# Where the tensor engine's operands begin in SBUF: every tile it reads is moved to 64 bytes past a multiple of 128

## The chip, the core and the metric

The kernel runs on one core of one Trainium2 chip. The core has a tensor engine (PE, whose weight loads the profile lists apart as PEld), VectorE (DVE), ScalarE (ACT), GpSimd (POOL) and SyncE (SP, here a queue that issues transfers). They run side by side and wait for each other through semaphores. SBUF is the on-chip memory of 128 partitions; a tile `[P, n]` takes n elements in every partition, at the same byte address in each. PSUM, in eight banks, takes what the tensor engine writes.

The metric is device time in microseconds (us). Before the change three runs took 1286.78, 1286.78 and 1286.92 us, so the median is 1286.78.

## The reference

An attention block and a gated feed-forward block read the same x, and a gate per token mixes them. Cut to what matters (S = 2048 tokens, D = 448, H = 16 heads of 28, F = 1792, all float32):

```python
g = sigmoid((x * gate_w).sum(-1, keepdims=True))
qkv = x @ wqkv                                  # D -> 3 D
scores = einsum("bhqd,bhkd->bhqk", q, k) * 28 ** -0.5
a = einsum("bhqk,bhkd->bhqd", softmax(scores), v) @ wo
gate = einsum("bsd,df->bsf", x, W_gate); up = einsum("bsd,df->bsf", x, W_up)
b = einsum("bsf,fd->bsd", gate * (gate > 0) * up, W_down)
out = g * a + (1 - g) * b
```

## The kernel before

**Numbers as a high and a low part.** The tensor engine multiplies in float32r here, a faster form of 4-byte operands that keeps fewer bits. Each float32 operand is therefore split into a rounded high part (ScalarE, or VectorE where `dve_high` is called) and the low rest (a subtraction on VectorE or GpSimd), and a product is summed from high x high, low x high and high x low. For the depth of 448 (three chunks of 128 and one of 64, in whose other 64 rows the low part is packed) that makes 11 matmuls for each output tile (`TERMS`).

**Stages.** Each engine's order of work is written out by hand.

1. Projections (first 150 us or so). `W` holds wqkv and the gate's column, split: seven rows of 1346 elements per partition, row a at byte 5384 a, which is 8 a past a multiple of 128. `qk` (line 337) uses 128 columns of W as weights and streams 512 tokens of X past them. `vproj` (line 355) holds 128 tokens of X as weights and streams 450 columns of W. Before them stand 11 warm-up matmuls on a tile of zeros, `warm` (lines 378 to 382). GpSimd then clears the padding columns of V (lines 390 to 392).
2. Attention with half of the feed-forward mixed in (to 1072 us). Strings of letters give the order of TensorE's work: `m` is a matmul of `smax` (line 181: scores for the row maximum that VectorE takes), `s` one of `scores` (line 207: the scores again, which ScalarE turns into exponentials in the tiles `P`), `x` one of `gu_mm` (line 506: gate and up, weights `wg`, moving X). Between two strings a block of `pv` (line 540) multiplies P by V: plain float32, 32 columns wide, two instructions for each product.
3. The end. The remaining gate and up products, `wout` (line 719: attention's output times `WO`) and `down` (line 764: hidden tiles `hh` times `WD`), each streaming 448 columns. 

**Where the tiles lie.** Pools are stacked in SBUF in the order in which they are opened, without gaps: from the low end `const`, `keep`, `vp`, then `qkv` (first stage), `att` (attention) or `ffn` (the end), and from the high end `fe`. The addresses of the program as built, in bytes of a partition:

| tiles that TensorE reads | used in line | begins at | past a multiple of 128 |
|---|---|---|---|
| X (in `keep`) | 337, 355, 506 | 17280, 25472 | 0 |
| V | 540 | 35840 | 0 |
| K, three of them | 181, 207 | 68608, 76800, 84992 | 0 |
| Q, three of them | 181, 207 | 101376, 109568, 117760 | 0 |
| P, eleven of them | 540 | 52224 to 183296 | 0 |
| W, row a | 337, 355 | 158720 + 5384 a | 8 a |
| wg, two of them | 506 | 192224, 199392 | 96 |
| WO, WD | 719, 764 | 35840, 56576 | 0 |
| on, hh | 719, 764 | 142592 and others | 0 |

A matmul reads a part of such a tile, and all of these parts lie a multiple of 128 bytes behind the tile's (or W's row's) beginning. The row maxima `m` (line 189, 16 small transposes) lie at 0 and 64 in turn.

Of the kernel before, what the change touches and what calls it, by code (L numbers as in the profile page):

```python
# [8 lines left out]
F32 = mybir.dt.float32  # L9
F32R = mybir.dt.float32r  # L10
BF16 = mybir.dt.bfloat16
# [7 lines left out]
P = 128  # L19
S = 2048  # L20
D = 448
# [7 lines left out]
TB = 512  # L29
# [2 lines left out]
SCALE = DH ** -0.5  # L32
VC = D + 2
NQ = 2 * D // P
WARM = 11

EARLY = (5, 5, 4, 4, 4, 3, 3, 3, 2, 2, 2, 2, 1, 1, 1, 1)
# [39 lines left out]
def gated_mix_kernel(ctx, tc, x, wq, wo, wgu, wd, out):  # L77
    nc = tc.nc
    ctx.enter_context(tc.manual_schedule(engines={ENG.PE, ENG.Activation, ENG.DVE, ENG.Pool, ENG.SP}))

    const = ctx.enter_context(tc.tile_pool(name="const", bufs=1))
    psum = ctx.enter_context(tc.tile_pool(name="psum", bufs=1, space=PSUM))
    dram = ctx.enter_context(tc.tile_pool(name="dram", bufs=1, space=DRAM))
    keep = ctx.enter_context(tc.tile_pool(name="keep", bufs=1))

    def f32(ap):
        return ap.bitcast(F32)
# [12 lines left out]
    def ps_x():  # L100
        return banks[turn("x", (4, 5))]
# [47 lines left out]
    V = vp.tile([P, 4, NK, 4, 32], F32, name="V")  # L149
# [63 lines left out]
    def xf(tb, b):  # L213
        return X[tb][b // 4][:, b % 4]
# [11 lines left out]


    with tc.tile_pool(name="qkv", bufs=1) as pa:
        W = pa.tile([P, 7, 2 * D + VC], F32R, name="W")

        def load_w(c):
            c0, c1 = c * 2 * GD, (c + 1) * 2 * GD if c < G + 1 else 2 * D + VC
# [5 lines left out]
        def split_w(wr, c0, c1):  # L238

            ways = [[(W[:, :, c0:c1], wr)]]  # L240
            if c0 < 2 * D:
                w, r = (ap.rearrange(f"p c {n} -> p c a j d", a=2, j=4)
                        for ap, n in ((W[:, :, c0:c1], "(j a d)"), (wr, "(a j d)")))
                ways = [[(w[:, :, a], r[:, :, a]) for a in range(2)]]
# [11 lines left out]
        def split_first(wr, xr):  # L256

            r = wr.rearrange("p c (a j d) -> p c a j d", a=2, j=4)
            w = W[:, :, :2 * GD].rearrange("p c (j a d) -> p c a j d", a=2, j=4)

# [50 lines left out]
        def ps_any(late=False):  # L311
            return (ps_x if late else turn("any", (ps_s, ps_s, ps_x, ps_x)))()

        def mix(n, among):

            k = len(among)
            for f, *a in among[k * n // NT:k * (n + 1) // NT]:
                f(*a)
# [5 lines left out]
        def st_tile(tb, c):  # L324
# [3 lines left out]
            if k < 15 and k % 5 > 2:  # L328
                return outs[k % 5 - 3]
            if c == NQ - 1 and tb == 0:  # L330
                return pair[0][:, 2:].bitcast(F32R)
            return pa.tile([P, 2, TB], F32R, name=f"st_{tb}_{c}", tag="st", bufs=3)

        def qk(tb, c, terms=TERMS, among=()):
            ps = ps_any(c == NQ - 1)
            for n, (a, b) in enumerate(terms):
                nc.tensor.matmul(ps, W[:, a, c * P:(c + 1) * P], xf(tb, b), start=(n == 0), stop=(n == NT - 1))  # L337
                mix(n, among)
            st = st_tile(tb, c)

            def send():
                act_high(st[:, 0], ps)
                low(st[:, 1], ps, st[:, 0])
                nc.gpsimd.dma_start(qk_d[:, c * P:(c + 1) * P, tb * TB:(tb + 1) * TB].rearrange("r d t -> d r t"),
                                    f32(st))


            sends.append(send)
            if (tb, c) != (0, NQ - 1):
                sends.pop()()  # L350

        def vproj(tb, t, among=()):
            ps = ps_any(tb == 0 and t > 1)
            for n, (a, b) in enumerate(TERMS):
                nc.tensor.matmul(ps[:, :VC], xf(tb, b)[:, t * P:(t + 1) * P], W[:, a, 2 * D:], start=(n == 0),  # L355
                                 stop=(n == NT - 1))
                mix(n, among)
            k = tb * 4 + t
            nc.scalar.activation(V[:, :, k, :, :DH], ps[:, :D].rearrange("p (g h d) -> p g h d", g=G, d=DH), AF.Copy)
            nc.scalar.activation(zt[:, k:k + 1], ps[:, D:D + 1], AF.Copy)  # L360
            if t == 3:
                for g in (2, 3):
                    nc.gpsimd.dma_start(v_d[g][:, k - 3:k + 1], V[:, g, k - 3:k + 1])
# [11 lines left out]
        x1 = load_x(1)  # L375


        warm = pa.tile([P, TB], BF16, name="warm")
        nc.vector.memset(warm, 0.0)
        ps = ps_x()  # L380
        for n in range(WARM):
            nc.tensor.matmul(ps, warm[:, :P], warm, start=True, stop=True)
# [38 lines left out]
        units = [(qk, 3, 1), (qk, 2, 2), (qk, 3, 2)]  # L421
        units += [(qk, tb, c) for c in range(3, NQ) for tb in range(NB - 1, -1, -1)]
        vs = [(vproj, tb, t) for tb in range(NB - 1, -1, -1) for t in range(4)]
        mixed = units[:2]
        units = units[2:]
# [43 lines left out]
    fe = ctx.enter_context(tc.tile_pool(name="fe", bufs=1, side="right"))  # L469
# [61 lines left out]
    OS, LS = {}, {}  # L531
# [24 lines left out]

    def spread(h):

        LS[h] = fe.tile([P, TB], F32, name=f"rb_{h}", tag="rb", bufs=1)
        for j in range(NB):  # L560
            nc.gpsimd.dma_start(LS[h][32 * j:32 * j + 32], l_d[h][j:j + 1].to_broadcast([32, TB]))

# [13 lines left out]
    def small_things(u):  # L576

        h, q = divmod(u, 4)

        if q == 0 and h and h + 2 < H:  # L580
            load_k(h + 2)
            load_q(h + 2)
        if u in (16, 32):
            g = u // 16 + 1
            nc.sync.dma_start(V[:, g % 2], v_d[g])
        if u == 2:
            pack_wo()
        if h and q == 2:
            row_sums(h - 1)
            spread(h - 1)  # L590
            summed.append(h - 1)
# [5 lines left out]
    for r, (order, nu) in enumerate(ROUNDS):  # L597
# [13 lines left out]
        for o in order:  # L611
# [16 lines left out]
            elif o == "x":  # L628
                i, half, k = passes.pop(0)
# [3 lines left out]
                if k == NT - 1:  # L633
                    i, half, ps = units.pop()
# [32 lines left out]
        for a in {i0, max(i0, (i0 + ni) // NK * NK)}:  # L667
            n = min(i0 + ni, (a // NK + 1) * NK) - a
# [132 lines left out]


    before(0, (spread, H - 1))
    before(1, (normalise, H - 1))
    for tb, load, split, at in ((0, 2, (3, 4), (5, 6, 7, 8)), (1, 5, (7, 9), (10, 11, 14, 14)), (2, 21, (23, 25), (28,) * 4),
                                (3, 35, (37, 39), (42,) * 4)):
        before(load, (fetch_o, tb))
        for k, i in enumerate(split):
            n = todo.index((down, i))
# [55 lines left out]
```

## Time and profile before

| | |
|---|---|
| median of the three runs | 1286.78 us |
| the profiled execution | 1284.91 us |
| its span, first to last instruction | 1283.1 us |
| instructions | 18205, of which 6687 matmuls |
| granted clock of TensorE | 1.000 |
| busy: PE, DVE, ACT, POOL | 100%, 70%, 61%, 29% of the span |

Each line of the groups by line names the source line, the engine, the operation, the tiles (written `out<-in`), the shapes and the count; then the busy time in us, the mean of one in ns, and the engine's idle time before them. The busy time of matmuls overlaps, since each begins before the last one has drained. The chain of work that ended last is followed back from the last instruction; in order of time each of its rows gives the start in us from the span's beginning, the length, and the engine and line that held the chain in that piece (`x22`: 22 instructions in a row).

### The profile page before, as it was taken

To read this page: it belongs to the slowest core of one execution; us is meant where nothing else is said; L and a number is where in the kernel's file an instruction comes from. 1 tells how busy PE (TensorE), PEld (TensorE's weight loads), DVE (VectorE), ACT (ScalarE), POOL (GpSimd) and SP (SyncE) were. 2 spreads that over 40 slices of the span, in tenths; PEclk is the share of its full clock that TensorE was granted. 3 is DMA by queue.
4 is the path that set the end of the run, shared out by engine and by line. 5 is a ranking of instruction groups with operands and counts; after the bars stand their busy time and mean duration, and the time that the engine had idled before them with its cause. 6 is when DMAs were issued, how large, how long until landed. Compare 5 with 4: busy or idle time off the path is not lost.

```text
span 1283.1 us, 18205 instructions
## 1 busy us (share of the span) xinstructions
PE 1277.6 (100%) x6687; PEld 922.8 (72%) x6687; DVE 895.1 (70%) x1364; ACT 777.0 (61%) x1424; POOL 370.4 (29%) x563
## 2 busy tenths in 40 slices
PE   9999999999999999999999999999999999999998
PEld 6888866677666676666766667766667666899997
DVE  6598768788777797777977778877779215663342
ACT  6212767687766786676867667766778773312121
POOL 3222222312323123323123331223231444551020
PEclk9999999999999999999999999999999999999999
DMA  9836443233144214231443423142331226634432
GB/s 321 290 151 244 133 137 86 71 79 98 60 132 146 74 43 114 71 103 50 116 119 120 109 70 77 43 115 66 108 105 36 83 83 204 218 109 135 143 104 78
DMA packets 53569, 148.89 MB, mean 116 GB/s; under 512 B 10024, under 2 KB 17128, under 8 KB 48872
## 3 DMA queue, kind: packets, MB, share of 16 engines
q1 hardware_dynamic: 36120, 98.34, 27.0%
q0 software_dynamic: 16928, 48.93, 10.6%
q8 instruction: 52, 0.85, 0.3%
q10 hardware_dynamic: 432, 0.46, 0.1%
q14 instruction: 37, 0.30, 0.1%
HBM read 102.06 MB, written 46.02 MB: 115 GB/s over the span
## 4 chain that ended last, share of the span: by engine, by line
PE 99%; DMA 0%; DVE 0%; issue 0%; ACT 0%; DVEq 0%
PE b L506 22%; PE b L207 19%; PE b L181 19%; PE b L540 17%; PE b L764 11%; PE b L337 5%; PE b L719 3%; PE b L355 3%; DMA wr<-wq 0%; PE b L189 0%; DVE W L129 0%; DVE X L129 0%; DVE y L770 0%; ACT X L123 0%; ACT W L123 0%
## 5 line engine op out<-in xcount | busy, mean ns | idle before, releaser
L182 DVE TENSOR_REDUCE mx<-b 128x1 f32<-128x512 f32 x1024 | 685.2, 688 | 27.5 <-PE b L181 20.4
L209 ACT ACTIVATE P<-b 128x512 f32<-128x512 f32 x840 | 493.0, 598 | 153.2 <-PE b L207 84.5
L506 PE MATMUL b<-X,wg 128*128 128x512 f32 (+1 forms) x1232 | 438.4, 400 | 0.0
L207 PE MATMUL b<-Q,K 114*128 114x512 f32 x1024 | 406.1, 397 | 0.0
L181 PE MATMUL b<-K,Q 112*128 112x512 f32 x1024 | 403.7, 397 | 0.0
L506 PEld LDWEIGHTS b<-X,wg 128*128 128x128 f32 (+1 forms) x1232 | 222.6, 189 | 58.0 <-issue 9.5
L207 PEld LDWEIGHTS b<-Q,K 114*128 114x128 f32 x1024 | 194.9, 190 | 53.1 <-issue 12.6
L181 PEld LDWEIGHTS b<-K,Q 112*128 112x128 f32 x1024 | 193.0, 189 | 49.1 <-DVE mx L182 2.6
L540 PE MATMUL b<-P,V 128*32 128x512 f32 x1680 | 188.2, 593 | 0.0
L132 POOL TENSOR_TENSOR wg<-wgr,wg 128x384 fp32r<-128x384 f32 x200 | 143.2, 732 | 9.8 <-issue 1.6
L764 PE MATMUL b<-WD,hh 128*128 128x448 f32 x672 | 141.1, 368 | 0.0
L540 PEld LDWEIGHTS b<-P,V 128*32 128x32 f32 x1680 | 52.6, 110 | 121.3 <-issue 118.7
L528 POOL DMA_DIRECT2D h_d<-h x56 | 31.4, 562 | 363.4 <-DVE h L522 311.7
L764 PEld LDWEIGHTS b<-WD,hh 128*128 128x128 f32 x672 | 126.1, 188 | 13.0
L209 ACT ACTIVATE V<-b 128x512 f32<-128x512 f32 x184 | 107.8, 599 | 41.3 <-PE b L207 26.7
L123 ACT ACTIVATE hh<-hr 128x512 fp32r<-128x512 f32 x56 | 35.2, 631 | 127.8 <-PE b L764 123.3
L129 DVE TENSOR_TENSOR hh<-hr,hh 128x512 fp32r<-128x512 f32 x56 | 50.7, 906 | 68.3 <-ACT hh L123 68.2
L337 PE MATMUL b<-X,W 128*128 128x512 f32 x308 | 84.1, 397 | 0.3 <-DVE X L129 0.2
L546 DVE TENSOR_TENSOR os<-b,os 128x512 f32<-128x512 f32 x16 | 11.1, 692 | 86.1 <-PE b L540 86.1
L337 PEld LDWEIGHTS b<-X,W 128*128 128x128 f32 x308 | 57.7, 189 | 15.3 <-DVE X L129 2.1
L555 POOL DMA_DIRECT2D l_d<-rs x16 | 9.0, 564 | 203.0 <-DVE rs L554 203.0
L544 DVE COPY os<-b 128x512 f32<-128x512 f32 x16 | 11.1, 691 | 78.5 <-PE b L540 78.5
(70 smaller groups left out, 709.8 us busy)
## 6 DMA issues: line engine op xcount, KB each, us to landing
wgr<-wgu SPq DMA_DIRECT2D x55, 512.0 KB
K<-qk_d SPq DMA_DIRECT2D x64, 224.0 KB
Q<-qk_d SPq DMA_DIRECT2D x64, 224.0 KB
h_d<-h POOLq DMA_DIRECT2D x56, 256.0 KB, 2.6
hr<-h_d SPq DMA_DIRECT2D x56, 256.0 KB
qk_d<-st POOLq DMA_DIRECT2D x21, 512.0 KB, 3.6
x_d<-X POOLq DMA_DIRECT2D x6, 1024.0 KB, 5.0
X<-x_d SPq DMA_DIRECT2D x24, 256.0 KB
```

What stands on the lines that cost most here:

```text
L129: nc.vector.tensor_tensor(dst, src, f32(high), op=OP.subtract)
L132: nc.gpsimd.tensor_tensor(dst, src, f32(high), op=OP.subtract)
L181: nc.tensor.matmul(ps, Q[h][:GD, u * P:(u + 1) * P], K[h % 3][:GD, c * TB:(c + 1) * TB], start=True, stop=True)
L182: nc.vector.tensor_reduce(MX[h][:, 4 * u + c:4 * u + c + 1], ps, axis=AX.X, op=OP.max)
L207: nc.tensor.matmul(ps, K[h % 3][:GD + 2, kt * P:(kt + 1) * P], Q[h][:GD + 2, j * TB:(j + 1) * TB], start=True, stop=True)
L209: nc.scalar.activation(PT[i][:, j], ps, AF.Exp, scale=SCALE)
L337: nc.tensor.matmul(ps, W[:, a, c * P:(c + 1) * P], xf(tb, b), start=(n == 0), stop=(n == NT - 1))
L355: nc.tensor.matmul(ps[:, :VC], xf(tb, b)[:, t * P:(t + 1) * P], W[:, a, 2 * D:], start=(n == 0), stop=(n == NT - 1))
L506: nc.tensor.matmul(ps, WS[i][rows, s, a], xf(i // NF, b)[rows], start=(n == 0), stop=(n == NT - 1))
L540: nc.tensor.matmul(po[32 * j:32 * j + 32], V[:, h // 4 % 2, i % NK, h % 4], p[:, j], start=(i == i0), stop=(i == i0 + ni - 1))
L719: nc.tensor.matmul(ps[:, :D], ON[tb][b // 4][:, b % 4, t * P:(t + 1) * P], WO[:, a], start=(n == 0), stop=(n == NT - 1))
L764: nc.tensor.matmul(ACC[i // NF][t][:, :D], HH[i][:, a, t * P:(t + 1) * P], WD[:, f, b], start=(f == 0 and n == 0), stop=(f == NF - 1 and n ...
```

## The change

No instruction is added, removed or put in another order. Four things change size or place:

- `const` gets a tile `pad` of 16 float32, 64 bytes, ahead of all others. Everything that is stacked from the low end moves up by 64 bytes: X, V, K, Q, P, WO, WD, on and hh begin at 64 past a multiple of 128.
- W's rows grow from 1346 to 1376 elements, 5504 bytes, which is 43 x 128. Every row then begins at 64. `vproj` names the 450 columns that it reads.
- `rb`, in the pool `fe`, is taken 8 elements longer. What is stacked from the high end moves down by 32 bytes, so wg goes from 96 to 64.
- `warm` has no tile of its own any more. It lies in the last quarter of V, which nothing has used yet at that time. Its size and type are as before. GpSimd's clearing of that quarter must now come behind the warm-up matmuls.

```diff
+WC = 1376
...
+    const.tile([P, 16], F32, name="pad")
...
-        W = pa.tile([P, 7, 2 * D + VC], F32R, name="W")
+        W = pa.tile([P, 7, WC], F32R, name="W")
...
-                nc.tensor.matmul(ps[:, :VC], xf(tb, b)[:, t * P:(t + 1) * P], W[:, a, 2 * D:], start=(n == 0),
+                nc.tensor.matmul(ps[:, :VC], xf(tb, b)[:, t * P:(t + 1) * P], W[:, a, 2 * D:2 * D + VC], start=(n == 0),
...
-        warm = pa.tile([P, TB], BF16, name="warm")
+        warm = V[:, 3, 0:2].rearrange("p k h d -> p (k h d)").bitcast(BF16)
...
-        LS[h] = fe.tile([P, TB], F32, name=f"rb_{h}", tag="rb", bufs=1)
+
+        LS[h] = fe.tile([P, TB + 8], F32, name=f"rb_{h}", tag="rb", bufs=1)[:, :TB]
```

## The prediction, made before the changed kernel ran

> **What bounds the kernel now.** I read the page's totals first, then the chain of work that ended last, then the groups of instructions by line and shape, and last the chain in order of time, piece by piece.
>
> ```profile
> span 1283.1 us, 18205 instructions
> ...
> PE 1277.6 (100%) x6687; PEld 922.8 (72%) x6687; DVE 895.1 (70%) x1364; ACT 777.0 (61%) x1424; POOL 370.4 (29%) x563
> ...
> PEclk9999999999999999999999999999999999999999
> ...
> PE 99%; DMA 0%; DVE 0%; issue 0%; ACT 0%; DVEq 0%
> PE b L506 22%; PE b L207 19%; PE b L181 19%; PE b L540 17%; PE b L764 11%; PE b L337 5%; PE b L719 3%; PE b L355 3%; DMA wr<-wq 0%; PE b L189 0%; DVE W L129 0%; DVE X L129 0%; DVE y L770 0%; ACT X L123 0%; ACT W L123 0%
> ```
>
> TensorE is the bound: 99% of the chain is matmuls, the clock is full in every slice, and no other engine is over 70%. So the time is the number of matmuls times the distance from one start to the next. A change that adds no instruction can move the time only by moving that distance. The counts come from the groups by line and shape:
>
> ```profile
> L506 PE MATMUL b<-X,wg 128*128 128x512 f32 x1136 | 421.9, 397 | 0.0
> L207 PE MATMUL b<-Q,K 114*128 114x512 f32 x1024 | 406.1, 397 | 0.0
> L181 PE MATMUL b<-K,Q 112*128 112x512 f32 x1024 | 403.7, 397 | 0.0
> L540 PE MATMUL b<-P,V 128*32 128x512 f32 x1680 | 188.2, 593 | 0.0
> L764 PE MATMUL b<-WD,hh 128*128 128x448 f32 x672 | 141.1, 368 | 0.0
> L337 PE MATMUL b<-X,W 128*128 128x512 f32 x308 | 84.1, 397 | 0.3 <-DVE X L129 0.2
> L355 PE MATMUL b<-W,X 128*128 128x450 f32 x176 | 46.9, 368 | 0.0
> L540 PE MATMUL b<-V 128*32 128x512 f32 x368 | 44.4, 593 | 0.0
> L719 PE MATMUL b<-WO,on 128*128 128x448 f32 x176 | 37.8, 368 | 0.0
> ```
>
> The mean of one (397 ns) is a latency with its modelled end, not the distance. The distance is read from the chain in order of time (start, length, what), where one matmul's piece ends at the next one's start. First a stretch of the main loop, between two blocks of L540:
>
> ```profile
> 165.23 9.58 PE b L540 x88
> ...
> 175.02 0.23 PE b L181
> ...
> 179.92 0.24 PE b L207
> ```
>
> Between these last two starts lie 21 matmuls of L181, L207 and L506: 4.90 us / 21 = **233.3 ns** each. Then runs of one line in other stages:
>
> ```profile
> 1085.46 5.15 PE b L506 x22
> ...
> 1191.49 9.09 PE b L719 x44
> 1200.58 34.72 PE b L764 x168
> ```
>
> L506: 5.15 / 22 = 234.1 ns. L719: 9.09 / 44 = 206.6 ns; L764: 34.72 / 168 = 206.7 ns. The last two stream 448 columns, the first 512: (233.3 - 206.6) / 64 = 0.417 ns a column. So 448 columns are 186.8 ns and 512 are 213.5 ns, and **19.8 ns of each matmul are not columns**. These 19.8 ns are all that an operand's place could touch.
>
> Almost every operand lies at 0 past a multiple of 128 bytes now (wg at 96). The exception is W, whose row a begins at 8a: L337 reads it as weights, L355 as the moving operand of 450 columns. That is the only place where the trace of before shows other starts:
>
> ```profile
> 29.97 7.62 PE b L337 x33
> 37.59 2.25 PE b L355 x11
> 39.84 2.53 PE b L337 x11
> 42.37 2.25 PE b L355 x11
> 44.62 2.53 PE b L337 x11
> 47.15 2.25 PE b L355 x11
> 49.40 2.53 PE b L337 x11
> ```
>
> L337: (7.62 + 3 x 2.53) / 66 = **230.5 ns**, 2.8 less than the main loop at the same 512 columns. L355: 3 x 2.25 / 33 = **204.5 ns**; L719's 206.6 with two more columns would be 207.4, so 2.9 less. Two lines with different roles for W (weights, moving) both stand about 2.9 ns under the lines whose operands begin on a multiple of 128. That is the one lead that the profile gives on the sign.
>
> **The change part by part.**
>
> *The pad in `const`, and `rb` 32 bytes longer.* No instruction. X, K, Q, P, V, WO, WD, hh and on go from 0 to 64, wg from 96 to 64. The lines with no W in them are L506 (1136), L207, L181 (1024 each), L764 (672) and L719 (176): 4032 matmuls. What a start at 64 costs stands in no row. Bounds: the nearest rows are W's starts, 8 to 48, at -2.9 ns with one operand off 128; with both off, as here, the two might add up, -5.8 ns. On the other side stands the extra piece that a start at 64 touches (second rival), up to +6.7 ns. I take -2.9: it is a measured distance on the same instruction kind, both roles show it, and that it adds is not shown. 4032 x 2.9 ns = **-11.7 us**; at -5.8 it is -23.4 us.
>
> The weights alone at 96 give nothing: L506's run at 234.1 ns stands 0.8 over the main loop's mean. That is the row that speaks against my value, and why the saving isn't counted twice.
>
> *W's rows padded from 1346 to 1376 elements.* Every row now starts at 64 in place of 8a: 308 + 176 = 484 matmuls. They are off 128 before and after, so 0; if they lost what they have, 484 x 2.9 = +1.4 us. The splits on ScalarE and VectorE that write W keep their shapes.
>
> *The 2048 instructions of L540.* P and V go from 0 to 64 as well. They stand at 9.58 / 88 = 109 ns a start, four at a time in the columns of the array, and no row shows another start. Taken as 0; in proportion to the others (2.9 of 233.3, 1.2%) their 2048 x 0.109 = 223 us would give or cost 2.8 us.
>
> *The 96 half-height matmuls of L506 and the 16 of L189*: by the same 2.9 ns, 0.3 us, left out.
>
> *`warm` moves into V.* Its memset is the same 128x256 words, but POOL's clearing of V must now come after the warm-up matmuls have read it:
>
> ```profile
> 0.87 0.27 DVE L379 MEMSET warm<- 128x256 uint32 x1 [0.87 <-PEq L858]
> ...
> 1.20 3.99 PE L382 MATMUL b<-warm 128*128 128x512 bf16 x11 [1.20 <-DVE warm L379]
> ...
> 4.98 0.32 POOL L391 MEMSET V<- 128x256 f32 x1
> ...
> 6.42 0.35 POOL L391 MEMSET V<- 128x256 f32 x1
> ...
> 12.01 0.89 POOL L344 DMA_DIRECT2D qk_d<-st  x1 [4.96 <-DVE st L129]
> ```
>
> The warm-up ends at 1.20 + 3.99 = 5.19 us; the memset of the quarter that it uses, the last of four, starts at 6.42. If the wait is kept for the whole tile, the first one moves from 4.98 to 5.19. Behind it on POOL stands the transfer at 12.01, after 4.96 us of idle time, which hides either; without that cover it would be 0.2 us. Cost 0.
>
> *Transfers.* Those that fill K, Q, X now land at 64. The first stage has nearly all of the wait on DMA, and its raw tiles wr and xr are read by the splits, not by TensorE. In the main loop the chain has no DMA piece, so a slower landing is hidden by the rows above. Cost 0.
>
> **Sum:** -11.7 us. The profiled execution, 1284.91 us with a span of 1283.1, would come to 1273.2. The median of the three runs, 1286.78, is 1.87 above it, so the forecast for the median is 1286.8 - 11.7 = **1275.1 us**, 0.9% faster.
>
> **The rivals.**
>
> *First: only the place of one operand relative to the other matters.* L337 and L355 would be quicker because their two operands begin at different distances from 128, and not because one of them is off 128. After the change all pairs begin alike again. Then 4032 matmuls keep their distance and W's 484 lose 2.9 ns, +1.4 us: 1288.2 us, or 1287.3 if wg, which now matches X, falls by the 0.8 ns of its row (1136 x 0.8 = -0.9). For it: both quick lines are mixed pairs. Against it: L506 at 96 against X at 0 is mixed too and stands at 234.1. The Trainium skill speaks against this rival (SBUF — State Buffer, section "Who interferes with whom"): the weights and the moving operand come through two independent read ports, and TensorE waits on no one; by that rule it would fall away, and no row here tests it.
>
> *A variant: the start within 128 does nothing at all*, and W's lines are quick for another reason of the first stage. 1286.8 us. A rule of the Trainium skill gives just this (Advanced Engine Details and Errata, section "Memory Cachelines"): SBUF's lines are 16 bytes, and what counts is the hits on a line. By it a start at 0, 64 or 96 is the same, and W at 8, 24 and 40 would be the worse one; the rows have W's lines quicker, so this trace doesn't bear the second half out. The case that a pad is swallowed by rounding belongs here too, at under 0.01: before has tiles at 64 (gate, every other m), so nothing rounds to 128.
>
> *Second, on the other side: a start at 64 reads one piece of 128 bytes more.* A moving row of 2048 bytes covers 16 such pieces from 0 and 17 from 64; 1792 bytes cover 14 and 15. If the stream has to wait for the broken first piece, half of one is 16 columns, 16 x 0.417 = 6.7 ns; if some of it is fetched ahead, less. Its place is each start of L337, L506, L207, L181, L764 and L719: 308 + 4032 = 4340 matmuls. At 6.7 ns that is +29.1 us, 1315.9 us. For it: 19.8 ns of each matmul are no columns, about one and a half such pieces, so starts do cost. Against it: weights of 512 bytes from 96 touch five pieces in place of four at 0.8 ns, and W's do at no cost. L355 can't test it, since 1800 bytes touch 15 pieces from 0 as from 8 to 48. Between 0.8 and 6.7 I take 3.3 ns: +14.3 us, **1301 us**. It decides from 0.6 ns a matmul on (2.6 us, 0.2%).
>
> **How the numbers follow.** Differences under 0.2% (2.6 us) can't be told from none here. Forecast, the saving of starts off 128: 0.56, between 1283 and the 1263.4 of both operands, with 1260.6 if L540 follows. First rival and its variant: 0.18, of which 0.14 within 0.2% and 0.04 slower, where W loses more than it had. Second rival: 0.26. So faster 0.56, same 0.14, slower 0.30. Predicted: 1275 us, the likeliest case; its own range is 1260 to 1283. For 8 in 10 the range must take in the first rival and the lower half of the second: **1257 to 1302 us**; under 1257 a saving beyond all rows would have to come (0.07), over 1302 the second rival above its middle price (0.13).
>
> **What would show each step.** In the chain by time, stretches of L181, L207 and L506 between blocks of L540 at some 230.4 ns in place of 233.3, and L764's run of 168 at 34.2 us in place of 34.72, bear the forecast out. If L764 stays at 34.72 and L337 rises to 233, it is the first rival. If L764's run comes to 35.3 us or more, it is the second: that run has no other change in it. Both operands adding up shows as 227.5 ns. If L540's blocks of 88 leave 9.58 us, its zero was wrong. POOL's first memset after 5.19 shows the new wait. The forecast is wrong if the time leaves 1260 to 1283, and its reason is wrong, even at the right time, if the main loop's distance hasn't moved and the gain stands elsewhere.

## The result, and the profile after

The change makes no difference that can be measured: over 14 runs of each kernel the median is 1285.61 us, before 1286.37 us, and the ratio of the means is 0.9998 with a 95% interval of 0.999 to 1.0007. The times of the changed kernel spread wider than those of before: 1283.2 to 1288.2 us against 1285.0 to 1287.3.

"No change" is here the sum of two changes. The chain of waits in order of time (start, length, what) of the changed kernel; L544 is before's L540, L510 its L506, L769 its L764 and L724 its L719:

```profile
165.70 9.58 PE b L544 x88
...
1065.57 9.58 PE b L544 x88
1075.15 10.21 PE b L510 x44
1087.79 5.04 PE b L510 x22
...
1157.39 34.04 PE b L769 x168
1191.44 8.92 PE b L724 x44
```

From before, the two rows that the prediction hadn't shown:

```profile
1062.91 9.58 PE b L540 x88
1072.49 10.50 PE b L506 x44
```

| | before | after | difference |
|---|---|---|---|
| start of the first block of P x V | 165.23 | 165.70 | +0.47 us |
| from there to the start of the last such block | 897.68 | 899.87 | +2.19 us |
| such a block of 88 | 9.58 | 9.58 | 0 |
| the last stage, from the end of that block to the end of the span | 210.61 | 206.25 | -4.36 us |
| span of the profiled execution | 1283.1 | 1281.4 | -1.7 us |

The table sets one profiled execution against another, and the changed kernel's, 1283.21 us, was the quickest of its 14.

The last stage's 448-column matmuls went from 206.7 to 34.04 / 168 = 202.6 ns (8.92 / 44 = 202.7 in L724), and its runs of L510 alone from 234.1 to 5.04 / 22 = 229.1 ns. In the main loop matmuls got slower. The trace's starts of consecutive matmuls show where: a matmul's distance to the next depends on which tile it streams and which weights are loaded meanwhile. Means over all such pairs in the main loop and the last stage, with the address of these weights less that of the moving operand, modulo 256:

```
streaming   weights of the next   count   distance: before, after   ns: before, after
K or Q      wg                     945        224, 128               233.0, 236.2
K or Q      Q or K                 921          0, 0                 234.5, 235.0
X           K or Q                 930        128, 128               233.4, 232.1
X           wg                     175         96, 0                 234.6, 230.5
hh's and on's 448-column lines     825          0, 0                 206.6, 202.7
```

In the first three rows the differences times the counts come to 3.0 + 0.5 - 1.2 = +2.3 us, the main loop's +2.19. Two of these rows kept their distance and changed all the same, so a pair's own distance is not all that counts.

### The profile page after: what moved, and what is told of

It reads as the page before. It is cut to its first block, busy times and chain, and to the rows that moved or that the text cites. A ratio compares the mean times of both kernels' runs of the same rounds, so it can differ in the third digit from the quotient of the medians.

```text
span 1281.4 us, 18203 instructions
## 1 busy us (share of the span) xinstructions
PE 1275.9 (100%) x6687; PEld 924.0 (72%) x6687; DVE 894.7 (70%) x1364; ACT 777.0 (61%) x1424; POOL 371.2 (29%) x563
## 4 chain that ended last, share of the span: by engine, by line
PE 99%; DMA 0%; DVE 0%; issue 0%; ACT 0%; DVEq 0%
PE b L510 22%; PE b L211 19%; PE b L185 19%; PE b L544 17%; PE b L769 11%; PE b L341 5%; PE b L359 3%; PE b L724 3%; DMA wr<-wq 0%; PE b L193 0%; DVE W L133 0%; DVE X L133 0%; DVE y L775 0%; ACT X L127 0%; ACT W L127 0%
## 5 line engine op out<-in xcount | busy, mean ns | idle before, releaser
L510 PE MATMUL b<-X,wg 128*128 128x512 f32 (+1 forms) x1232 | 436.1, 398 | 0.0
L510 PEld LDWEIGHTS b<-X,wg 128*128 128x128 f32 (+1 forms) x1232 | 222.3, 189 | 58.0 <-issue 9.6
L544 PE MATMUL b<-P,V 128*32 128x512 f32 x1680 | 188.2, 593 | 0.0
L544 PEld LDWEIGHTS b<-P,V 128*32 128x32 f32 x1680 | 52.6, 110 | 121.2 <-issue 118.7
L769 PE MATMUL b<-WD,hh 128*128 128x448 f32 x672 | 138.5, 365 | 0.0
L769 PEld LDWEIGHTS b<-WD,hh 128*128 128x128 f32 x672 | 126.3, 188 | 10.2
L133 DVE TENSOR_TENSOR hh<-hr,hh 128x512 fp32r<-128x512 f32 x56 | 45.9, 819 | 66.2 <-ACT hh L127 66.1
L341 PE MATMUL b<-X,W 128*128 128x512 f32 x308 | 83.9, 398 | 0.3 <-DVE X L133 0.3
L341 PEld LDWEIGHTS b<-X,W 128*128 128x128 f32 x308 | 58.4, 190 | 14.3 <-DVE X L133 1.1
```

What stands on the lines that cost most here:

```text
L133: nc.vector.tensor_tensor(dst, src, f32(high), op=OP.subtract)
L510: nc.tensor.matmul(ps, WS[i][rows, s, a], xf(i // NF, b)[rows], start=(n == 0), stop=(n == NT - 1))
L544: nc.tensor.matmul(po[32 * j:32 * j + 32], V[:, h // 4 % 2, i % NK, h % 4], p[:, j], start=(i == i0), stop=(i == i0 + ni - 1))
L769: nc.tensor.matmul(ACC[i // NF][t][:, :D], HH[i][:, a, t * P:(t + 1) * P], WD[:, f, b], start=(f == 0 and n == 0), stop=(f == NF - 1 and n ...
```

## The experiments

**Streams with nothing else at work.** Two kernels made only of matmuls, one source line for each case.

```diff
+    def ops(m, w, cols):            # m, w: bytes by which the two operands are put later
+        for n in range(66):
+            c, a = n % 4, n % 7
+            yield (banks[...][:, :cols], wt[:, w // 4 + a * P:w // 4 + (a + 1) * P],
+                   mv[:, m // 4 + c * 512:m // 4 + c * 512 + cols], n % 11 == 0, n % 11 == 10)
+    for o, l, r_, s, e in ops(0, 64, 512): nc.tensor.matmul(o, l, r_, start=s, stop=e)
```

> Leaves out the whole computation: it only streams matmuls of float32r, 66 in a row for each pair of starts (moving operand at 0, 32, 64, 96 past a multiple of 128; weights at 0, 32, 64, 96), at 512 and at 448 columns, each pair twice, in opposite orders, with no other engine at work. Before the change the stage-three stretches stood at 206.7 ns (448 columns, both at 0) and the main loop at 233.3 (512 columns, both at 0); after it L769 stands at 202.7 ns (448, both at 64). A (the prediction's step: a start off 128 saves a fixed 2.9 ns for each operand): 512 columns fall from 233.3 at (0, 0) to 230.4 with one operand off and 227.5 with both; 448 columns from 206.7 to 203.8 and 200.9. B (only the distance between the two starts matters): the pairs (0, 0), (32, 32), (64, 64), (96, 96) are all alike, 233.3 and 206.7, and the others lower. C (the two streams fall into a repeating pattern that depends on both starts, on the columns and on how the run began): 448 columns show 206.7 at (0, 0) and 202.7 at (64, 64), 512 columns show differences of up to 10 ns that don't follow those of 448, and the two visits of one pair can differ. D (the start does nothing; the 4 ns of the last stage come from elsewhere): every pair 233.3 and 206.7.

The starts are counted from each tile's own beginning. The weights' tile begins 128 past the moving one's, modulo 256, so (0, 0) is a distance of 128 in the next table and (0, 64) one of 192. Rows of its chain. L55 is (moving at 0, weights at 64), L57 (32, 0), L60 (32, 96), L61 (64, 0), L62 (64, 32), L63 (64, 64), L66 (96, 32), L67 (96, 64), all at 512 columns; L71 is (0, 64) and L76 (32, 96) at 448; L132 is the second visit of (0, 0) at 512:

```profile
43.42 15.12 PE b L55 x66
...
73.94 15.45 PE b L57 x66
...
120.12 15.11 PE b L60 x66
135.24 15.40 PE b L61 x66
150.64 15.45 PE b L62 x66
166.09 15.33 PE b L63 x66
...
212.21 15.40 PE b L66 x66
227.61 15.45 PE b L67 x66
...
285.47 13.20 PE b L71 x66
...
352.95 13.21 PE b L76 x66
...
1149.10 15.40 PE b L132 x66
```

A length divided by 66 is the distance between starts. (0, 64) and (32, 96) agree at 229.0 ns, (64, 0) and (96, 32) at 233.3, (32, 0), (64, 32) and (96, 64) at 234.1. So the absolute start does nothing, and A falls: (64, 64) is 232.3 where A had 227.5, and (0, 0) 233.3. What counts is how far the weights lie behind the moving operand. B had that, but also that unequal starts are quicker, and most stand at 233.3 to 234.1. +64 and -64 differ, so the period is longer than 128.

> Leaves out the whole computation, as starts_table does. The moving operand stays on one address (0 past a multiple of 512), and the weights begin at 0 to 480 bytes further (steps of 32, with 176 and 208), at 512 and at 448 columns, 66 matmuls each, each twice. In starts_table pairs with the same distance of weights behind moving operand gave the same distance between matmuls whatever the absolute start (0/64 and 32/96: 229.0 and 229.0; 64/0 and 96/32: 233.4 and 233.4; 32/0, 64/32, 96/64: 234.2 each), but +64 and -64 differ, so the period isn't 128. B (the distance of the two starts decides, with a period of 256): each pair 256 bytes apart in this table agrees within 0.3 ns, with the dip to 229.0 (512) and 200.0 (448) at the distance that starts_table had there (192, and 448 again). B512 (a period of 512): only one of the two dips. C (the run's beginning decides as well): the two visits of one distance differ by 2 ns and more at several distances. Last, a copy of the last stage's own order (weights changed twice in three matmuls, moving operand 0, 1792, 0; 448 columns; 132 in a row) with both tiles at 0, both at 64, and weights 64 or 192 behind, or 64 ahead: by A (the absolute start) 206.7 with both at 0 and 202.7 with both at 64; by B these two are alike, and one of the others lies at 200 to 202; by C the two visits of one of them differ.

In its chain L72 and L141 are the two visits of distance 192 at 512 columns, L74 is 256, L80 448, L147 the second visit of 0. At 448 columns L84 and L129 are the two visits of 0, L87 is 96 and L90 192. L102 and L103 are the last stage's order with both tiles at 0 and both at 64, L105 with the weights 192 behind, L110 the second visit of both at 64:

```profile
105.84 15.12 PE b L72 x66
...
136.37 15.00 PE b L74 x66
...
228.41 15.12 PE b L80 x66
...
289.41 13.63 PE b L84 x66
...
329.87 13.22 PE b L87 x66
...
370.10 13.20 PE b L90 x66
...
531.38 26.75 PE b L102 x132
558.13 26.75 PE b L103 x132
...
611.57 26.40 PE b L105 x132
...
743.88 27.28 PE b L110 x132
...
1207.86 15.41 PE b L141 x66
...
1300.24 14.98 PE b L147 x66
```

The whole table, in ns from start to start (the first visit of 0 at 512 is left out: its first dozen matmuls stand 427 ns and more apart, at a granted clock of 1.00):

| weights behind the moving operand, modulo 256 | 0 | 32 | 64 | 96 | 128 | 160 | 192 | 224 |
|---|---|---|---|---|---|---|---|---|
| 512 columns | 227.0 to 227.3 | 233.3 | 233.3 | 234.1 | 233.4 or 232.3 | 233.4 | 229.1 or 233.4 | 233.3 |
| 448 columns | 206.5 or 202.7 | 204.4 | 202.2 | 200.2 | 204.0 | 205.3 | 200.0 | 206.7 |

Distances 256 apart agree (L74 with L147, L80 with L72), which bears out B. At some distances there are two values, which bears out C: at 0 and 448 columns 206.5 in one visit (L84) and 202.7 in the other. The first is what the last stage had before the change, the second what it has after. (In starts_table 448 columns at distance 96 have two as well: 206.4 in one visit, 200.0 to 200.3 in five.) The last stage's own order shows both too: 26.75 / 132 = 202.7 with both tiles at 0 and with both at 64, and 27.28 / 132 = 206.7 in the second visit of both at 64 (L110). The start of the tiles doesn't choose between them.

A rule of the Trainium skill would have every start that is a multiple of 16 alike (Advanced Engine Details and Errata, "Memory Cachelines": lines of 16 bytes). The table doesn't agree: multiples of 32 span 227.0 to 234.1 ns. Another rule of the Trainium skill (SBUF — State Buffer, "Who interferes with whom": two independent read ports, TensorE waits on no one) doesn't fit either as a statement on time, since the place of one operand relative to the other decides up to 7 ns of each matmul. Why the period is 256 no run shows.

**The last stage's tiles alone.**

```diff
+    pf.tile([P, 16], F32, name="pad")
     WO = pf.tile([P, 7, D], F32R, name="WO")
```

> Only the pool of the last stage gets 64 bytes of padding ahead of WO, so WO, WD, on and hh begin at 64 past a multiple of 128; all else stays as before. A (the absolute start of both operands): L764's runs of 168 fall from 34.72 us to the 34.05 of the whole change, the last stage by 4 us, and the kernel to 0.997 of before, since the main loop, which lost 2.7 us in the whole change, isn't touched. B and C (the distance between the operands, which is unchanged here, and what pattern the stage falls into at its start): no fixed answer from the start at 64; the runs of 168 stay at 34.7 us, or stand at another of a few fixed values, and the ratio is 0.997 to 1.000.

The ratio was 0.9974 (0.996 to 0.9987), and the run of 168 matmuls:

```profile
1155.66 34.05 PE b L765 x168
```

That is A's number, and taken alone it would have settled on the wrong cause. The pad also changed the distances at which the stage's streams follow those of L506: hh behind X from 128 to 192, wg behind WD from 224 to 160. The next kernel changes such distances without touching WD and hh.

**The whole change's distances without its pad.**

```diff
-        LS[h] = fe.tile([P, TB], F32, name=f"rb_{h}", tag="rb", bufs=1)
+        LS[h] = fe.tile([P, TB + 24], F32, name=f"rb_{h}", tag="rb", bufs=1)[:, :TB]
```

> rb grows by 96 bytes and nothing else changes, so wg comes to 128 past a multiple of 256 and stands to X, K, Q, WD and hh at exactly the distances (modulo 256) that the whole change gave it: X 0, K and Q 128, WD 128. All other tiles lie where they were before, at 0 past a multiple of 128; W's rows stay at 8a. Distance, with the way a stretch is entered (B and C): the kernel repeats the whole change without its pad: the main loop ends 2 to 3 us later than before (1074.5 to 1075.5 us in place of 1072.5), the runs of L506 alone fall from 5.15 to 5.04 us for 22, L764's runs of 168 fall to 34.05 us although neither WD nor hh was moved, and the ratio is 0.998 to 1.000. Absolute start (A): WD and hh are where they were, so 34.72 us, and the main loop ends at 1072.5.

The ratio was 0.9988 (0.9979 to 0.9998), and the chain repeats the changed kernel almost piece by piece, with every tile but wg (and rb, which TensorE doesn't read) where it was before:

```profile
1065.51 9.58 PE b L540 x88
1075.09 10.21 PE b L506 x44
...
1087.73 5.04 PE b L506 x22
...
1157.59 34.04 PE b L764 x168
```

The last block starts at 1065.51 (1065.57 after, 1062.91 before), the run takes 34.04 us. This shows that the distances are what the change did, to the main loop's loss and the last stage's gain alike; that the stage gains without WD and hh being moved shows that it depends on what stands before and between its runs. Nor is it wg's own start: the next kernel, fe_only, puts wg at the very start that the change gave it (192 past a multiple of 256) but at other distances, and its runs of 168 stay at 34.72 us.

**What keeps the main loop from the low values.** wg alone, and all pairs at distance 0:

```diff
# fe_only
+        LS[h] = fe.tile([P, TB + 8], F32, name=f"rb_{h}", tag="rb", bufs=1)[:, :TB]
# loop0
+    const.tile([P, 32], F32, name="pad")
+    vp.tile([P, 32], F32, name="pad2")
     K = [vp.tile([P, S], F32R, name=f"K{r}") for r in range(3)]
+        warm = V[:, 3, 0:2].rearrange("p k h d -> p (k h d)").bitcast(BF16)
+        LS[h] = fe.tile([P, TB + 56], F32, name=f"rb_{h}", tag="rb", bufs=1)[:, :TB]
```

> Only rb grows by 32 bytes, so the weights wg go from 96 to 64 past a multiple of 128, and all else stays as before: W's rows at 8a, the rest at 0. By the distance modulo 256, weights wg behind a moving K or Q go from 224 to 192, behind X from 96 to 64. B: by starts_table's values at these distances the pair 'K or Q moving, wg next' falls from 233.4 to 229.0 and 'X moving, wg next' from 234.2 to 233.4; there are some 950 of the first and 250 of the second among L181, L207 and L506, so the main loop gets 4 us shorter and the kernel 0.997 of before. A: the weights go from one start off 128 to another, no change, 1.000. C: the pattern of a stretch depends on all of its neighbours, between 0.997 and 1.002.

> X, K, Q and wg are all put on a multiple of 256 (distance 0 for every pair in the main loop), by pads of 128 bytes ahead of X and of K and 224 bytes in the pool of wg; warm goes into V for room; the last stage keeps its distance of 0. Distance (B): distance_table has 227.0 ns at distance 0 and 512 columns, where the main loop now stands at 233.3; its 3184 matmuls of L181, L207 and L506 would fall by up to 6.3 ns, 20 us, 0.984 of before. If the pattern is broken at each change from one line to the next (C), most stays near 233 and only the runs of L506 alone (22 in a row) go from 5.15 to 5.0 us: 0.998 to 1.000. Absolute start (A): X, K, Q stay on a multiple of 128, wg comes to 0 too: no gain, 1.000 or a little slower. The last stage: runs of 168 at 34.72 or 34.05 us, by chance.

fe_only came out at 0.9994 (0.9985 to 1.0004) and its last block of P x V ended at 1073.25 us, 0.8 later than before: B's 4 us are missing. loop0 came out at 0.9986 (0.9977 to 0.9996), its block ended at 1074.15 us, 1.7 later than before. Its runs of L506 alone fell to 5.04 us for 22, and its last stage, still at distance 0, to 34.04 us for 168: the gain is in the last stage alone. The table's values don't carry over to the mixed loop. The next kernel looks for what breaks them.

> Leaves out the whole computation. Three streams in turn, as L181, L207 and L506 stand in the main loop: three moving tiles and three weight tiles, 512 columns, 132 matmuls a case, each case twice. At distance 0 throughout: with sums of 11, with each result of the first two streams on its own in a bank, with 112, 114 and 128 rows as in the kernel, and with VectorE's maximum and ScalarE's exponential reading these banks. Then with the distances of before (X 128, wg 224 past a multiple of 256, the rest 0) and of the whole change (64, 64, 192; weights 64, 64, 192), plain and with the readers. B (distance alone): 227.0 ns at distance 0 in each of the four cases. C with the readers or the rows as what breaks the pattern: 227.0 in the plain cases and 233 to 234 from the case on that has what breaks it. C with the change of tile itself as what breaks it: 233 to 234 in all four. Before's distances against the change's, with readers: in the main loop they stood at 233.3 and 234.1 or so; the same order here bears out that the distances alone made the loop longer.

Rows of its chain: L69 and L82 distance 0 with 128 rows, L70 and L81 the same with 112, 114 and 128 rows, L71 with the readers as well; L74 and L77 the distances of before with rows and readers, L75 and L76 those of the change:

```profile
49.99 29.92 PE b L69 x132
79.91 30.81 PE b L70 x132
110.72 30.86 PE b L71 x132
...
202.46 30.79 PE b L74 x132
233.25 31.04 PE b L75 x132
264.29 31.10 PE b L76 x132
295.39 30.81 PE b L77 x132
...
418.41 30.80 PE b L81 x132
449.21 29.93 PE b L82 x132
```

Three streams in turn keep 29.92 / 132 = 226.7 ns, so changing the tile breaks nothing. With 112 and 114 partitions in place of 128 it is 30.81 / 132 = 233.4, and the readers add under 1 ns. In the kernel's own form the change's distances are 1.9 to 2.2 ns slower than those of before (31.04 and 31.10 against 30.79 and 30.81), the sign that the main loop showed.

**A version that beats both.** The last stage's weights 192 behind; then loop0 with it:

```diff
     WD = pf.tile([P, NF, 2, D], F32R, name="WD")
+    pf.tile([P, 48], F32, name="pad")
```

> Only the last stage's weights hh and on are put 192 bytes further behind the moving WD and WO, by a pad after WD; every moving operand stays at 0 past a multiple of 128, and all else as before. Distance (B): at 192 distance_table has 200.0 ns at 448 columns, in both visits and in the last stage's own order; L764's runs of 168 fall from 34.72 to 33.6 us, the last stage's 848 matmuls by 6.6 ns each, 5.6 us, the kernel to 0.9956 of before, and its times no longer fall into two groups 4 us apart, since 200.0 has no second pattern. Absolute start (A): the moving operand is where it was and the weights are at 64, so at most the saving of one operand, 2.9 ns or 2.5 us, 0.998. Start does nothing (D): 1.000.

> loop0 and tail192 together. Distance (B): the two savings add, 20 + 5.6 us, 0.980 of before. C: 0.994 to 0.9956, the last stage's part alone. A: 1.000.

tail192 came out at 0.9957 (0.9942 to 0.9972), its run of 168 at 33.60 us, 200.0 ns:

```profile
1157.04 33.60 PE b L765 x168
```

B's number, from weights moved against an unmoved WD. Its five times still spread, from 1278.9 to 1281.3 us. both came out at 0.9973 (0.996 to 0.9986): loop0's distances add nothing (1281.53 us against tail192's 1279.57). C had that they wouldn't, but its range ended at 0.9956. Then the rows:

```diff
+        nc.sync.dma_start(f32(Q[h])[GD:P], z_d)        # z_d: zeros in DRAM, written once
-        nc.tensor.matmul(ps, Q[h][:GD, u * P:(u + 1) * P], K[h % 3][:GD, c * TB:(c + 1) * TB], start=True, stop=True)
+        nc.tensor.matmul(ps, Q[h][:, u * P:(u + 1) * P], K[h % 3][:, c * TB:(c + 1) * TB], start=True, stop=True)
-        nc.tensor.matmul(ps, K[h % 3][:GD + 2, kt * P:(kt + 1) * P], Q[h][:GD + 2, j * TB:(j + 1) * TB],
+        nc.tensor.matmul(ps, K[h % 3][:, kt * P:(kt + 1) * P], Q[h][:, j * TB:(j + 1) * TB],
```

> both (distance 0 in the main loop, 192 in the last stage), and L181 and L207 take all 128 partitions of K and Q in place of 112 and 114: rows 112 to 127 of Q are filled with zeros from DRAM with each load, so the products are the same. loop_alone at distance 0 stood at 226.7 ns with 128 rows and at 233.3 with 112 and 114, with or without readers. Rows and distance together (E): the 3184 matmuls of the main loop fall to 227 ns or so where no wait breaks in, 15 to 20 us with the last stage's 5.6: 0.980 to 0.986 of before, if the 16 more loads and rows hide. If the readers or the waits break the pattern as well: 0.9956 to 0.9975, as both. If the zeros' loads come late: slower than both, with waits of L181 on Q.

> The same 128 rows, but with the main loop's distances as they were before (X to K and Q 128, wg 224 or 96), moved together by 128 bytes, and tail192's last stage. E (the low pattern needs both the rows and distance 0): the main loop stays between 230.1 and 233.3, which loop_alone had at these distances with 128 rows: 0.990 to 0.9956 of before, behind rows128. If the rows alone decide: as rows128.

rows128 has a median of 1271.25 us, 0.9894 (0.9877 to 0.991), and is the fastest kernel here; rows_before 0.9933 (0.9918 to 0.9947). In rows128 the last block of P x V starts 8.6 us earlier than before, and the last stage is tail192's:

```profile
1054.34 9.70 PE b L548 x88
...
1146.88 33.60 PE b L773 x168
```

So full rows pay with both sets of distances that were tried, and more with distance 0: rows_before against tail192 is 1276.77 against 1279.57 us, rows128 against both 1271.25 against 1281.53. E's size was too large: 0.9894 lies outside its 0.980 to 0.986, and the mean of 512 columns in rows128's main loop came to 230.5 ns, not 227. What breaks the pattern in the rest wasn't tried.

**The changed kernel again**, unaltered:

> The changed kernel once more, unaltered: its 14 times lay between 1283.2 and 1288.2 us, and the profiled execution was the fastest. If a stretch settles by chance in one of several patterns, a second profile shows other lengths for the same stretches: L769's runs of 168 at 34.72 in place of 34.05 us (then the last stage is 4 us longer), or a main loop that ends some us from 1075.15. If the pattern is fixed by the addresses, both stand as in the first profile, and the spread of the times comes from elsewhere. Ratio to before 0.999 to 1.0007, as measured.

The ratio was 1.0002 (0.9991 to 1.0012). The stretches were those of the first profile (the last block starts at 1065.46, runs of 34.05 us). But the span was 1283.0 in place of 1281.4 us, and the difference stands in one place, at the start of the last stage. The timeline there (the bracket holds idle time and what ended it):

```profile
1089.01 4.74 DVE L130 CAST WD<-wdr 128x448 fp32r<-128x448 f32 x1
1090.39 4.37 POOL L136 TENSOR_TENSOR WO<-wor,WO 128x1344 fp32r<-128x1344 f32 x2
...
1096.77 1.45 PE L510 MATMUL b<-X,wg 128*128 128x512 f32 x5 [1.39 <-DVE wg L133]
```

A cast of VectorE that takes 0.37 us elsewhere lasts 4.74 us here. It begins 1.4 us ahead of GpSimd's subtraction for WO and ends 0.3 us behind the first of that one's two instructions (1090.39 + 3.10). The split of wg behind it comes late, and TensorE stands idle. In the first profile the long one was the split of wg itself, without a wait; before the change it was one for hh, with a wait of 0.02 us. The end of the cast is in line with the Trainium skill (SBUF — State Buffer, "Who interferes with whom": VectorE and GpSimd share a pair of ports that one of them holds for a whole instruction); why a cast that began first waits, the trace doesn't show. This is the 1.6 us between these two executions. The rest of the wider spread stays open. Both profiled executions had the quicker last stage, and whether the slowest ones had it no profile shows.

## Why the prediction was wrong, step by step

The prediction's value rests on one stretch of L337 in the trace of before. Later in that trace the same line, with the same starts of W, stands at the main loop's distance:

```profile
55.37 0.70 PE b L337 x3
...
56.31 0.70 PE b L337 x3
...
57.24 0.70 PE b L337 x3
```

That is 2.10 / 9 = 233.3 ns. From 52 us on, the trace's starts give a mean of 233.2 ns over 143 matmuls of L337, against 230.5 in the stretch that was read.

- *TensorE sets the time, and 19.8 ns of each matmul are not columns.* Right. The table's lows (227.0 at 512, 200.0 at 448) take a third of them away.
- *"I take -2.9: it is a measured distance on the same instruction kind, both roles show it."* This step failed. The 2.9 ns came from one stretch, 30 to 52 us, and didn't hold for the rest of the same line, as the rows above show. And what the stretch had was read as the price of a start off 128. In starts_table both operands at 64 cost what both at 0 cost (232.3 and 233.3, the two values of distance 128), and weights at 8, 16, 24 and 48, which are starts of W's rows, gave 233.3, 233.3, 231.1 and 230.2 ns (L85 to L88): no fixed saving. W's rows lie at other distances from X, 8 bytes more with each row; whether these made the stretch quick wasn't tried. After the change the stretch takes (7.91 + 3 x 2.53) / 67 = 231.3 ns (230.5 before), though every row of W begins at 64, which is 128 or 0 behind X, modulo 256.
- *The sum.* 4032 x 2.9 ns took one sign for all. In the profiled executions it was -4.0 ns on the 448 columns (34.72 to 34.04 us for 168), where -2.9 was the forecast, and a gain of some 9 us forecast for the main loop came out as a loss of 2.2 us.
- *L540 at zero.* Right: 9.58 us for 88 before and after.
- *W padded, at zero.* Near enough: L341 as said; L359's three runs of 11 take 2.26 us in place of 2.25.
- *warm at zero.* Right. POOL's first clearing of V starts at 4.97 us (4.98 before), so the wait goes by quarters, and the last one stands at 6.41 (6.42).
- *First rival: the place of one operand relative to the other.* The right variable. It had 0.18 together with its variant, since L506 at 96 seemed to speak against it. It counted modulo 128, by which all pairs begin alike again; modulo 256 wg came to 128 behind K and Q, not to 0. And equal distances were to give equal times: the last stage kept its distance of 0 and gained 4 ns, because two patterns exist there. Its 1287 to 1288 us is 2 above the median.
- *Its variant: the start within 128 does nothing at all.* Its 1286.8 us came nearest to the median, by luck: the start of a tile does nothing by itself, but the change moved distances, and a gain and a loss happened to cancel.
- *Second rival: one piece of 128 bytes more.* Refuted: (64, 64) is no slower than (0, 0), 15.33 against 15.40 us for 66.
- *What would show it.* L764 at 34.2 us or less was named as the forecast's sign, and the profile showed 34.04. The sign was too weak: it couldn't tell the start from the distance. The main loop's 230.4 ns, the other sign, was absent.

## What to carry to other kernels

Where TensorE alone sets the time, the place of the next weights relative to the operand being streamed, modulo 256 bytes, is worth a table for the column count in use; the start of either by itself isn't. Such values held here in long runs of one kind with all 128 partitions in use, so fill the rows before tuning the distances, and test a stage in the kernel, not only in the table. When a change with no net effect comes up, compare the stages before calling it nothing: here, in the profiled executions, -4.4 and +2.7 us stood behind 0.9998. And before a distance is taken from one stretch, read the same line wherever else it stands.

## What was not expected of the hardware

- A matmul with 112 or 114 partitions is slower to follow than one with 128: 233.4 against 226.7 ns at distance 0 (loop_alone). At the distances of before, 128 rows gave 230.1 in one visit and 233.3 in the other.
- A stream can keep one of two speeds for a hundred matmuls and more with nothing different in its own addresses: 206.5 or 202.7 ns at 448 columns and distance 0. What chooses between them, beyond what stood before, stays open.
